# Delta-rule attention and two MLP stages on one core: output products held over the group boundary, untransposed triangles, a Newton square root and a block-wise first inversion

## The chip, the cores and the metric

The kernel runs on one core of one Trainium2 chip. TensorE (PE), VectorE (DVE), ScalarE (ACT), GpSimd (POOL) and the DMA queue of SyncE (SP) work side by side and wait for each other through semaphores. The metric is the device time of one execution in microseconds; of several runs the median is taken.

## The reference, cut to what matters

The inputs are q, k and v of 4 batches x 8 heads x 768 steps x 48 numbers, and a factor beta per step. The attention is a delta rule with a 48x48 state per head; its output goes through a gated MLP (384 to 1536 to 384, SiLU gate) and then a second MLP (384 to 2048 to 384, ELU):

```
k_n = k / (norm(k) + 1e-6)
for t in range(768):
    y[t]  = q[t] @ state
    state = state + beta[t] * outer(k_n[t], v[t] - k_n[t] @ state)
x   = y as [3072, 384]
x   = (silu(x @ w_gate) * (x @ w_val)) @ w_out
out = elu(x @ w_in) @ w_out2
```

## The kernel before, in words

**Groups.** The 3072 tokens are cut into 12 groups of 256: two batches x 128 steps, so 16 (batch, head) pairs `u` of 128 steps each. The 128 steps lie on the 128 partitions as four chunks `c` of 32. Inside a chunk the delta rule is solved at once: with A the strictly lower triangle of -beta k k^T, (I - A) is inverted for all 16 x 4 chunks, and only the states go from chunk to chunk.

**Attention of a group**, by function: `norm` (L162) squares k on POOL into `ain`, sums, and takes 1/(norm + 1e-6) with a Sqrt on ACT, a Newton-like correction and two reciprocals on DVE; `nkn` scales k by it. `trans` (L195) transposes q and k on PE, `kb` (POOL) scales k by -beta into `gr`, `gram` (L203) multiplies them and masks the result into `gr`. `inversion` (L219) transposes the triangles into `ain` in 32x32 blocks, eliminates row by row over 31 levels on DVE (L248 multiplies, L255 adds, a large level cut in two), transposes back into `ain` (`back`, L263), and copies the four chunks by ACT into `zt` (L270), where two 32x32 blocks stand on the diagonal of a 64x64 one. `xstep` (L276) multiplies by these inverses: 32 products of 64x64 with 96 columns. `gstep` (L286) makes the factors of the chunks in all four banks `at0` to `at3`, emptied by ACT (L298) and DVE (L299); `chain` carries the states, `yall` and `xtr` give the group's x in two parts `xh` and `xl`.

**First MLP of a group.** `gv1(g, f)` (L461) for the 12 slices f: 18 matmuls (L445) into one of the two banks `gv`, SiLU on ACT (L466), a multiply on DVE (L467) into `tb`, and a split into a high and a low part `hb` (ACT L345, DVE L348). `out1(g, f)` (L473) adds the slice to the one accumulator `acc` with 9 matmuls (L479); after slice 11 ACT empties `acc` (L486) into two `hb` buffers, from where DMAs write `x2d`.

**Order.** `moe1` (L611) writes the group's list: `out1` comes `LAG` = 2 slices after its `gv1`, and what is held at the end of a group is flushed there. `merge` (L590) mixes that list with the attention of the next group (and the inversion of the one after it), by the weights that stand with each step; what attention has goes over the first `ATT` = 0.85 of the list. The framework's planner then lays out each engine's queue, where a step that is ready in its model goes ahead of one that isn't; on the chip each engine works its queue in order. Group 0 has its attention, and the decoding of its weights (`decode`, integer and bit work on ACT, DVE and POOL), ahead of any MLP work. The second MLP (`h2`, `out2`) follows group 11; `t2` names the buffers in which its weights are decoded.

Of the kernel before, what the change touches and what calls it, by code (L numbers as in the profile page):

```python
# [11 lines left out]
I32 = mybir.dt.int32  # L12
# [9 lines left out]
def delta_moe_kernel(ctx: ExitStack, tc: tile.TileContext, q, k, v, beta,  # L22
# [9 lines left out]
    nc = tc.nc  # L32
# [28 lines left out]
    xl = {}  # L61
    NHB = 3
    NTB = 2

    ident = T("ident", [128, 128])
    strict = T("strict", [128, 32])
    zd = T("zd", [128, 2, 16])
    nbt = T("nbt", [128, NI, B * H])
# [10 lines left out]
    sm = [T(f"sm{n}", [128, 16]) for n in range(5)]  # L79
    neg1 = T("neg1", [128, 1])  # L80
# [24 lines left out]
    def emit_consts():  # L105
        make_identity(nc, ident)
        V.memset(neg1, -1.0)
        G.memset(strict, 1.0)
        for r in range(4):
            s = strict[32 * r:32 * r + 32, :]  # L110
            G.affine_select(out=s, in_=s, compare_op=ALU.is_ge, fill=0.0, base=-1,
                            pattern=[[1, 32]], channel_multiplier=-1)

        fl = sm[0][:, 0:1]
        V.tensor_reduce(out=fl, in_=ident.rearrange("p (r h m) -> p h r m", r=4, h=2)[:, 1],
                        op=ALU.add, axis=AX.XY)

        V.tensor_copy(zd[:, 1, :], fl.to_broadcast([128, 16]))
        V.tensor_scalar(out=zd[:, 0, :], in0=zd[:, 1, :], scalar1=-1.0, scalar2=1.0,
                        op0=ALU.mult, op1=ALU.add)  # L120

    def emit_zero():
        V.memset(kp[:, :, D:64], 0.0)
        V.memset(qp[:, :, D:64], 0.0)
        G.memset(zt, 0.0)
        G.memset(st[0:32], 0.0)
# [35 lines left out]
    def norm(g):  # L162
        i, b0 = ax_of(g)
        sq = ain[:, 0:768].rearrange("p (u d) -> p u d", d=D)
        ss, s, r, t, w = sm
# [15 lines left out]
    def nkn(g, a):  # L181
        u = slice(a * 8, a * 8 + 8)
        kk = kp[:, u, 0:D]
        V.tensor_tensor(out=kk, in0=kk, in1=sm[4][:, u].unsqueeze(2).to_broadcast([128, 8, D]),
                        op=ALU.mult)
        A.copy(out=R[:, u, 0:D], in_=kk)
# [31 lines left out]

    def inversion():  # L219
        lst = []  # L220
        an = ain.rearrange("p (l j) -> p l j", l=32)

        def start(n):
            def f():
# [3 lines left out]
                if n == 0:  # L228
                    z = buf['z'] = TT("z", [128, 32, 16])
                    G.memset(z, 0.0)  # L230
                    V.tensor_copy(win(z[:, 0:1, 0:1], [[16, 2], [33, 16]]), zd)
            return f
        lst += [start(n) for n in (3, 2, 1, 0)]

        def step(l):
            c0 = l // 2
# [19 lines left out]
            return [mul, add]  # L256
        for l in range(31, 0, -1):
            lst += step(l)

        def back():  # L260
            z = buf['z']
            t = ain[:, 0:512]
            V.transpose(out=t.rearrange("p (u i two) -> p i two u", u=16, two=2),  # L263
                        in_=z.rearrange("p a i -> p i a"))
        lst.append(back)

        def spread(r):
            def f():
                q0 = slice(32 * r, 32 * r + 32)
                A.copy(out=zt[q0, :, 32 * (r % 2):32 * (r % 2) + 32],  # L270
                       in_=ain[q0, 0:512].rearrange("p (u i) -> p u i", u=16))
            return f
        return lst + [spread(r) for r in range(4)]
# [280 lines left out]
    def attention(g, nx):  # L554
# [22 lines left out]
        if nx + 1 < NB:  # L577
            st1.append((0, lambda: load_q(nx + 1)))
        inv = inversion()
        inv = [(INV / len(inv), x) for x in inv]  # L580
# [30 lines left out]
    def moe1(g, before, after):  # L611
# [20 lines left out]
    POOL = 0  # L632
    CUT = 40
    LAG = 2
    LAG2 = 2
# [44 lines left out]
    def emit_all():  # L680
# [10 lines left out]
        for n in range(6, NW - 2):  # L691
            first.insert(1 + n - 6, (0, lambda n=n: load_w(n, src1(n))))
        inv = inversion()
        buf['dt'] = TT("dt", [128, 2, 2, DM], I32)
# [26 lines left out]
        late = []  # L721
        t2 = ("gr", "st", "zt", "dt")

# [64 lines left out]
```

## Time and profile before

| what | value |
|---|---|
| three runs | 1307.21, 1311.82 and 1316.99 us (median 1311.82) |
| profiled execution, first to last instruction (its span) | 1301.1 us |
| median less that span | 10.7 us |
| PE busy, PEld busy, DVE busy, ACT busy, POOL busy | 1162.0, 1078.5, 821.8, 608.6, 129.9 us |
| TensorE clock granted, mean | 0.949 |
| first MLP begins, group 11 ends, last instruction | 88.3, 880.9, 1301.1 us |

The profile gives no time of its own for the profiled execution beside its span, so the median stands in for it. The busy shares are averages over very different stages: 88 us of attention and decoding without MLP work, groups 0 to 11 up to 880.9 us, and the second MLP. They don't say which wait ends last in a stage; the rows below do.

### The profile page before, as it was taken

What the parts mean: (1) busy time and instruction counts of PE and PEld (TensorE: products, weight loads), DVE (VectorE), ACT (ScalarE), POOL (GpSimd) and SP (SyncE); (2) the same over time, 40 slices, a digit from 0 to 9 for tenths busy, and PEclk for the clock granted to TensorE, in tenths of its full rate; (3) what the DMA queues carried; (4) which work ended last, traced back from release to release, by engine and by line L of the source; (5) the groups of instructions that cost most, each with busy time, mean ns of one, the idle gap of its engine ahead of it and who ended that gap; (6) DMA issues with size and microseconds to landing.
All of it is one profiled execution on the core that took longest, in us unless ns stands there. A gap on an engine that the chain in (4) does not pass through costs nothing.

```text
span 1301.1 us, 31342 instructions
## 1 busy us (share of the span) xinstructions
PE 1162.0 (89%) x13086; PEld 1078.5 (83%) x13086; DVE 821.8 (63%) x2709; ACT 608.6 (47%) x1181; POOL 129.9 (10%) x106
## 2 busy tenths in 40 slices
PE   2473999898989898989898989989899999999998
PEld 1363889898888898989888989978689899899897
DVE  6799585848484858585848574467964545454443
ACT  7554534343425252535353524457754545454443
POOL 4353100000000000000000000031300000000000
PEclk9866798889999999999999999989999999999999
DMA  9530202020202020202020100373010101000000
GB/s 298 160 81 1 38 14 39 13 39 10 43 2 51 2 50 2 51 2 50 7 46 2 26 11 5 125 251 104 1 49 1 49 1 49 1 33 1 25 1 25
DMA packets 106815, 57.16 MB, mean 44 GB/s; under 512 B 76945, under 2 KB 101521, under 8 KB 106673
## 3 DMA queue, kind: packets, MB, share of 16 engines
q1 hardware_dynamic: 106672, 55.16, 16.7%
q8 instruction: 102, 1.67, 0.5%
q14 instruction: 41, 0.33, 0.1%
HBM read 45.71 MB, written 9.44 MB: 42 GB/s over the span
## 4 chain that ended last, share of the span: by engine, by line
PE 57%; DVE 34%; ACT 4%; issue 3%; DMA 1%; POOL 1%; SPq 0%; DVEq 0%; ACTq 0%; POOLq 0%
PE gv L445 14%; DVE z L255 7%; DVE ain L248 7%; PE acc L531 7%; PE at L531 7%; PE at L514 7%; PE gv L514 7%; PE acc L479 5%; PE at L294 4%; DVE w L404 2%; PE at L281 2%; DVE hb L348 2%; DVE tb L467 2%; DVE ain L227 2%; PE at L312 2%
## 5 line engine op out<-in xcount | busy, mean ns | idle before, releaser
L445 PE MATMUL gv<-xh,w 128*128 128x256 f32 x1728 | 295.9, 295 | 23.6 <-DVE tb L467 22.9
L445 PEld LDWEIGHTS gv<-xh,w 128*128 128x128 f32 x1728 | 248.9, 200 | 29.4 <-DVE tb L467 24.0
L479 PE MATMUL acc<-hb,w 128*128 128x256 f32 x1296 | 194.9, 298 | 37.6 <-ACT hb L345 34.7
L479 PEld LDWEIGHTS acc<-hb,w 128*128 128x128 f32 x1296 | 172.2, 199 | 45.5 <-ACT hb L345 36.7
L445 PE MATMUL gv<-xl,w 128*128 128x256 f32 x864 | 160.6, 295 | 1.5 <-DVE xl L348 1.5
L466 ACT ACTIVATE tb<-gv 128x256 f32<-128x256 f32 x144 | 54.9, 382 | 216.4 <-PE gv L445 216.0
L467 DVE TENSOR_TENSOR tb<-gv,tb 128x256 f32<-128x256 f32 x144 | 60.7, 422 | 127.6 <-ACT tb L466 126.7
L445 PEld LDWEIGHTS gv<-xl,w 128*128 128x128 f32 x864 | 131.7, 202 | 2.9 <-DVE xl L348 1.7
L345 ACT CAST hb<-tb 128x256 fp32r<-128x256 f32 x144 | 58.4, 406 | 146.8 <-DVE tb L467 146.2
L255 DVE TENSOR_TENSOR z<-z,ain 128x60 f32<-128x60 f32 (+32 forms) x696 | 122.5, 214 | 1.3
L248 DVE TENSOR_TENSOR ain<-z,ain 128x60 f32<-128x60 f32 (+32 forms) x696 | 122.3, 207 | 1.2
L348 DVE TENSOR_TENSOR hb<-tb,hb 128x256 fp32r<-128x256 f32 x144 | 76.7, 533 | 42.7 <-ACT hb L345 41.3
L521 DVE SCALAR_TENSOR_TENSOR hb<-at,hb 128x512 f32<-128x512 f32 x48 | 33.2, 691 | 84.5 <-ACT hb L520 84.5
L521 DVE SCALAR_TENSOR_TENSOR hb<-gv,hb 128x512 f32<-128x512 f32 x48 | 33.1, 690 | 80.2 <-ACT hb L520 72.5
L294 PE MATMUL at<-gr,R 32*96 32x80 f32 x1536 | 75.3, 276 | 8.7 <-DVE w L299 4.4
L294 PEld LDWEIGHTS at<-gr,R 32*96 32x96 f32 x1536 | 64.9, 179 | 19.0 <-DVE w L299 4.6
L520 ACT ACTIVATE hb<-hb,neg 128x512 f32<-128x512 f32 x96 | 69.4, 723 | 2.8
L518 ACT ACTIVATE hb<-at 128x512 f32<-128x512 f32 x48 | 28.6, 595 | 87.6 <-PE at L514 87.6
L518 ACT ACTIVATE hb<-gv 128x512 f32<-128x512 f32 x48 | 28.6, 596 | 85.3 <-PE gv L514 85.0
L281 PE MATMUL at<-R,zt 64*64 64x96 f32 x768 | 38.6, 254 | 27.5 <-ACT zt L270 27.4
L519 ACT ACTIVATE hb<-hb 128x512 f32<-128x512 f32 x96 | 60.6, 632 | 2.7
L281 PEld LDWEIGHTS at<-R,zt 64*64 64x64 f32 x768 | 35.8, 140 | 29.7 <-ACT zt L270 28.2
(174 smaller groups left out, 2154.6 us busy)
## 6 DMA issues: line engine op xcount, KB each, us to landing
w<-in_moe_w_out_dram SPq DMA_DIRECT2D x28, 384.0 KB, 6.6
w<-in_moe_w_in_dram SPq DMA_DIRECT2D x16, 384.0 KB, 5.6
kp<-in_k_dram SPq DMA_DIRECT2D x12, 384.0 KB, 5.4
qp<-in_q_dram SPq DMA_DIRECT2D x12, 384.0 KB, 4.3
w<-in_moe_w_gate_dram SPq DMA_DIRECT2D x12, 384.0 KB, 7.8
w<-in_moe_w_val_dram SPq DMA_DIRECT2D x12, 384.0 KB, 8.0
R<-in_v_dram SPq DMA_DIRECT2D x24, 192.0 KB, 2.6
x2d<-hb SPq DMA_DIRECT2D x12, 256.0 KB, 2.1
```

What stands on the lines that cost most here:

```text
L248: V.tensor_tensor(out=t, in0=z[:, l:l + 1, x:y].to_broadcast([128, l, y - x]), in1=an[:, l, 0:l].unsqueeze(2).to_broadcast([128, l, y - x] ...
L255: V.tensor_tensor(out=z[:, 0:l, x:y], in0=z[:, 0:l, x:y], in1=t, op=ALU.add)
L281: nc.tensor.matmul(p[r:r + 64, j], lhsT=zt[r:r + 64, 4 * n + j, :], rhs=R[r:r + 64, 4 * n + j, :], start=True, stop=True, skip_group_check ...
L294: nc.tensor.matmul(ps_[c][0:96, s * 80:s * 80 + 80], lhsT=R[t, u, :], rhs=gr[t, u, 0:80], start=True, stop=True, skip_group_check=True)
L348: (e2 or V).tensor_tensor(out=lo, in0=src, in1=hi.bitcast(F32), op=ALU.subtract)
L445: nc.tensor.matmul(dst, lhsT=wt[:, a_, kk * 128:(kk + 1) * 128], rhs=xx[:, kk, :], start=(n == 0), stop=(n == 3 * KD - 1))
L467: V.tensor_tensor(out=s, in0=p[:, TB:2 * TB], in1=s, op=ALU.mult)
L479: nc.tensor.matmul(o, lhsT=w[:, a_, d * 128:(d + 1) * 128], rhs=hh[:, b_, :], start=(f == 0 and n == 0 and d != 1), stop=(f == F1 - 1 and ...
L514: nc.tensor.matmul(p, lhsT=W[f][:, 0, a_, kk * 128:(kk + 1) * 128], rhs=x2[n][b_][:, kk, :], start=(m == 0), stop=(m == 3 * KD - 1))
L520: A.activation(out=r, in_=r, func=ACTF.Identity, bias=neg1, scale=1.0)
L521: V.scalar_tensor_tensor(out=r, in0=p, scalar=0.0, in1=r, op0=ALU.max, op1=ALU.add)
L531: nc.tensor.matmul(ob4[t], lhsT=hh[:, b_, t * 128:(t + 1) * 128], rhs=w[:, a_, :], start=(f == 0 and m == 0), stop=(f == F2 - 1 and m == 2))
```

## The change

1. **Held products.** `moe1` flushes what it holds only in the last group. So `out1(g, 10)` and `out1(g, 11)` now stand in group g + 1, behind its slices 0 and 1, and `acc` is emptied there. `NHB` is 4 in place of 3, for the slices that are live over the boundary.
2. **Inverted triangles where they stand.** `back` already leaves the inverses in `ain`, one 32x32 block for each of the 64 chunks; `zt` becomes a view of `ain`, the four copies (L270) and the clearing of the old `zt` go, and `xstep` makes 64 products of 32x32 in place of 32 of 64x64. `norm`, which writes `ain`, now has to wait for `xstep`.
3. **Newton square root.** The Sqrt on ACT goes; DVE starts from an integer guess and makes three Newton steps: 13 small DVE instructions in place of 6.
4. **Block-wise inversion in group 0.** There the two 16x16 halves of each triangle are inverted in the same 15 levels (30 instructions in all), and the part under them comes from two products on PE (`join1`, `join2`) with a DVE step between and an ACT copy behind.
5. **Smaller things.** `zd` is two columns in place of 32, `eye` holds four 32x32 identities, and the decode buffers `t2` are three in place of four.

```diff
-    NHB = 3
+    NHB = 4
...
-    zt = T("zt", [128, 16, 64])
+    zt = ain[:, 0:512].rearrange("p (u j) -> p u j", u=16)
...
     def norm(g):
...
-        A.activation(out=s, in_=ss, func=ACTF.Sqrt)
-
-        V.tensor_scalar(out=r, in0=s, scalar1=1e-18, scalar2=None, op0=ALU.max)
-        V.reciprocal(out=r, in_=r)
-        V.tensor_tensor(out=t, in0=ss, in1=r, op=ALU.mult)
-        V.tensor_tensor(out=t, in0=t, in1=s, op=ALU.add)
-        V.tensor_scalar(out=t, in0=t, scalar1=-0.5, scalar2=-1e-6, op0=ALU.mult, op1=ALU.add)
-        V.reciprocal(out=w, in_=t)
+        V.tensor_scalar(out=s.bitcast(I32), in0=ss.bitcast(I32), scalar1=-0.5,
+                        scalar2=float(0x5f3759df), op0=ALU.mult, op1=ALU.add)
+        for _ in range(3):
+            V.scalar_tensor_tensor(out=r, in0=s, scalar=-0.5, in1=ss, op0=ALU.mult, op1=ALU.mult)
+            V.tensor_tensor(out=r, in0=r, in1=s, op=ALU.mult)
+            V.scalar_tensor_tensor(out=s, in0=r, scalar=1.5, in1=s, op0=ALU.add, op1=ALU.mult)
+        V.tensor_tensor(out=r, in0=ss, in1=s, op=ALU.mult)
+        V.tensor_scalar(out=r, in0=r, scalar1=-1.0, scalar2=-1e-6, op0=ALU.mult, op1=ALU.add)
+        V.reciprocal(out=s, in_=r)
...
+        def halves(l):
+            c0 = l // 2
+            n = 8 - c0
+            t = win(ain[:, 512:513], [[8, 2], [32, l], [1, n]])
+
+            def mul():
+                z = buf['z']
+                V.tensor_tensor(out=t, in0=win(z[:, l:l + 1, c0:c0 + 1], [[264, 2], [0, l], [1, n]]),
+                                in1=win(ain[:, 32 * l:32 * l + 1], [[528, 2], [1, l], [0, n]]),
+                                op=ALU.mult)
+
+            def add():
+                z = win(buf['z'][:, 0:1, c0:c0 + 1], [[264, 2], [16, l], [1, n]])
+                V.tensor_tensor(out=z, in0=z, in1=t, op=ALU.add)
+            return [mul, add]
+        for l in range(15 if blocked else 31, 0, -1):
+            lst += (halves if blocked else whole)(l)
 
         def back():
...
+            if blocked:
+                V.transpose(out=d1t, in_=d1)
+
+        def join1():
+            p = buf['jp'] = nxt(atb, "at").rearrange("p (u j) -> p u j", u=16)
+            for u in range(16):
+                for c in range(C):
+                    r = 32 * c
+                    nc.tensor.matmul(p[r:r + 32, u],
+                                     lhsT=gr[r:r + 16, u, 80:112],
+                                     rhs=d1t[r:r + 16, u], start=True, stop=True,
+                                     skip_group_check=True)
+            v = buf['v'] = TT("z", [128, 16, 32])
+            V.scalar_tensor_tensor(out=v, in0=p, scalar=low[:, 0:1],
+                                   in1=eye.unsqueeze(1).to_broadcast([128, 16, 32]),
+                                   op0=ALU.mult, op1=ALU.add)
+
+        def join2():
+            p = nxt(atb, "at").rearrange("p (u j) -> p u j", u=16)
+            for u in range(16):
+                for c in range(C):
+                    t = slice(32 * c, 32 * c + 32)
+                    nc.tensor.matmul(p[t, u], lhsT=buf['v'][t, u], rhs=d1[t, u], start=True,
+                                     stop=True, skip_group_check=True)
+            A.copy(out=zt, in_=p)
+        return lst + ([back, join1, join2] if blocked else [back])
...
     def xstep():
         for n in range(4):
             p = nxt(atb, "at")[:, 0:384].rearrange("p (n w) -> p n w", n=4)
             for j in range(4):
-                for r in (0, 64):
-                    nc.tensor.matmul(p[r:r + 64, j], lhsT=zt[r:r + 64, 4 * n + j, :],
-                                     rhs=R[r:r + 64, 4 * n + j, :], start=True, stop=True,
+                for c in range(C):
+                    t = slice(32 * c, 32 * c + 32)
+                    nc.tensor.matmul(p[t, j], lhsT=zt[t, 4 * n + j, :],
+                                     rhs=R[t, 4 * n + j, :], start=True, stop=True,
                                      skip_group_check=True)
             A.copy(out=R[:, 4 * n:4 * n + 4, :], in_=p)
...
-        while held:
+        while held and g == NB - 1:
             put(1, held.pop(0), 1.0, out1)
...
-        t2 = ("gr", "st", "zt", "dt")
+        t2 = ("gr", "st", "dt")
```

## Rows read from the trace of the kernel before

**Rows 1.** Page, part 1: busy time of each engine, its share, instructions.
```profile
PE 1162.0 (89%) x13086; PEld 1078.5 (83%) x13086; DVE 821.8 (63%) x2709; ACT 608.6 (47%) x1181; POOL 129.9 (10%) x106
```
**Rows 2.** Stretches, groups 6, 10, 11: width; PE, PEld, DVE, ACT, POOL busy; clock; DMA.
```profile
516.90:581.50 64.60, 60.03 (x922) 56.96 (x922) 43.97 (x193) 26.63 (x63) 4.62 (x6) 0.97 0.15 27
...
776.20:829.00 52.80, 52.71 (x760) 50.44 (x761) 20.36 (x57) 18.04 (x48) 0.00 (x0) 0.97 0.03 9
829.00:880.90 51.90, 46.04 (x357) 45.06 (x356) 31.56 (x41) 26.62 (x49) 11.14 (x6) 0.93 0.76 253
```
**Rows 3.** PE in order of time, group 6 and its end: start, us, count, [idle].
```profile
523.94 2.86 PE L281 MATMUL at<-R,zt 64*64 64x96 f32 x64
...
574.65 2.67 PE L479 MATMUL acc<-hb,w 128*128 128x256 f32 x18
...
581.53 2.41 PE L479 MATMUL acc<-hb,w 128*128 128x256 f32 x9 [4.09 <-ACT hb L345]
...
588.68 2.86 PE L281 MATMUL at<-R,zt 64*64 64x96 f32 x64
```
**Rows 4.** Chain of waits at that end: start, us, what.
```profile
576.98 1.08 DVE ain L263
...
578.77 0.63 ACT zt L270
579.41 0.38 ACT tb L466
```
**Rows 5.** PE's waits, 186 to 780 us: for whom, total, times, longest.
```profile
PE acc L479 <- ACT hb L345: 33.5, 9, 4.1
```
**Rows 6.** Chain of waits: gv products behind the first and last end; undisturbed ones.
```profile
255.54 5.13 PE gv L445 x35
...
778.34 7.04 PE gv L445 x53
...
865.77 2.16 PE gv L445 x18
```
**Rows 7.** PE in order of time, group 6: factors, transposes, triangles.
```profile
529.06 0.92 PE L294 MATMUL at<-gr,R 32*96 32x80 f32 x32
...
543.04 1.03 PE L200 MATMUL at<-ident,qp 128*128 128x128 f32 x8
543.91 1.04 PE L200 MATMUL at<-ident,kp 128*128 128x128 f32 x8
...
549.15 1.73 PE L210 MATMUL at<-kq 48*32 48x64 f32 x128
```
**Rows 8.** Groups of instructions: busy, mean ns | idle before, releaser.
```profile
L201 ACT COPY kq<-at 128x512 f32<-128x512 f32 x48 | 25.7, 588 | 0.7 <-DVE tb L467 0.5 <-PE at L200 0.3
...
L166 POOL TENSOR_TENSOR ain<-kp 128x768 f32<-128x768 f32 x11 | 16.1, 1465 | 18.8 <-ACT zt L270 18.8
...
L168 ACT ACT_TABLE_LOAD x11 | 14.1, 1283 | 0.2
...
L248 DVE TENSOR_TENSOR ain<-z,ain 128x60 f32<-128x60 f32 (+32 forms) x696 | 122.3, 207 | 1.2
...
L521 DVE SCALAR_TENSOR_TENSOR hb<-at,hb 128x512 f32<-128x512 f32 x48 | 33.2, 691 | 84.5 <-ACT hb L520 84.5
```
**Rows 9.** DVE in order of time in group 0's attention.
```profile
12.83 0.18 DVE L170 TENSOR_SCALAR sm<-sm 128x16 f32<-128x16 f32 x1 [4.91 <-ACT sm L168]
...
14.25 1.03 DVE L184 TENSOR_TENSOR kp<-kp,sm 128x384 f32<-128x384 f32 x2
...
28.13 0.19 DVE L248 TENSOR_TENSOR ain<-z,ain 128x31 f32<-128x31 f32 x1
...
43.68 1.06 DVE L263 STREAM_TRANSPOSE ain<-z 128x512 f32<-128x512 f32 x1
```
**Rows 10.** PE in order of time in group 0's attention.
```profile
17.18 2.73 PE L210 MATMUL at<-kq 48*32 48x64 f32 x128 [0.34 <-ACT kq L201]
46.87 6.34 PE L281 MATMUL at<-R,zt 64*64 64x96 f32 x64 [26.95 <-ACT zt L270]
```

More of the change, by code (lines that the diff above doesn't have):

```diff
@@ L66, in delta_moe_kernel @@
     strict = T("strict", [128, 32])
-    zd = T("zd", [128, 2, 16])
+    zd = T("zd", [128, 2])
     nbt = T("nbt", [128, NI, B * H])
@@ L75, in delta_moe_kernel @@
     ain = T("ain", [128, 1024])
-    zt = T("zt", [128, 16, 64])
+    zt = ain[:, 0:512].rearrange("p (u j) -> p u j", u=16)
+    eye = T("eye", [128, 32])
+    low = zd[:, 1:2]
     st = T("st", [128, B, DM])
     sv = T("sv", [128, 2, C - 1, DM])
-    sm = [T(f"sm{n}", [128, 16]) for n in range(5)]
+    sm = [T(f"sm{n}", [128, 16]) for n in range(3)]
     neg1 = T("neg1", [128, 1])
@@ L112, in emit_consts @@
                             pattern=[[1, 32]], channel_multiplier=-1)
-        fl = sm[0][:, 0:1]
-        V.tensor_reduce(out=fl, in_=ident.rearrange("p (r h m) -> p h r m", r=4, h=2)[:, 1],
+        for r in range(4):
+            q0 = slice(32 * r, 32 * r + 32)
+            V.tensor_copy(eye[q0], ident[q0, q0])
+        V.tensor_reduce(out=low, in_=ident.rearrange("p (r h m) -> p h r m", r=4, h=2)[:, 1],
                         op=ALU.add, axis=AX.XY)
-        V.tensor_copy(zd[:, 1, :], fl.to_broadcast([128, 16]))
-        V.tensor_scalar(out=zd[:, 0, :], in0=zd[:, 1, :], scalar1=-1.0, scalar2=1.0,
+        V.tensor_scalar(out=zd[:, 0:1], in0=low, scalar1=-1.0, scalar2=1.0,
                         op0=ALU.mult, op1=ALU.add)
@@ L124, in emit_zero @@
         V.memset(qp[:, :, D:64], 0.0)
-        G.memset(zt, 0.0)
         G.memset(st[0:32], 0.0)
@@ L183, in nkn @@
         kk = kp[:, u, 0:D]
-        V.tensor_tensor(out=kk, in0=kk, in1=sm[4][:, u].unsqueeze(2).to_broadcast([128, 8, D]),
+        V.tensor_tensor(out=kk, in0=kk, in1=sm[1][:, u].unsqueeze(2).to_broadcast([128, 8, D]),
                         op=ALU.mult)
@@ L216, in gram, with inversion @@
                         op=ALU.mult)
-    def inversion():
+    def inversion(blocked):
         lst = []
         an = ain.rearrange("p (l j) -> p l j", l=32)
+        d1 = ain[:, 0:512].rearrange("p (u j) -> p u j", u=16)
+        d1t = ain[:, 512:1024].rearrange("p (u j) -> p u j", u=16)
         def start(n):
@@ L230, in f, with whole @@
                     G.memset(z, 0.0)
-                    V.tensor_copy(win(z[:, 0:1, 0:1], [[16, 2], [33, 16]]), zd)
+                    V.tensor_copy(win(z[:, 0:1, 0:1], [[16, 2], [33, 16]]),
+                                  zd.unsqueeze(2).to_broadcast([128, 2, 16]))
             return f
         lst += [start(n) for n in (3, 2, 1, 0)]
-        def step(l):
+        def whole(l):
             c0 = l // 2
@@ L256, in step @@
             return [mul, add]
-        for l in range(31, 0, -1):
-            lst += step(l)
-        def back():
[L261 to L272, printed above, removed]
@@ L273, in inversion @@
-        return lst + [spread(r) for r in range(4)]
+        def halves(l):
[11 more added lines that the diff above has]
+            return [mul, add]
@@ new lines, in inversion @@
+        for l in range(15 if blocked else 31, 0, -1):
+            lst += (halves if blocked else whole)(l)
+        def back():
+            V.transpose(out=ain[:, 0:512].rearrange("p (u i two) -> p i two u", u=16, two=2),
+                        in_=buf['z'].rearrange("p a i -> p i a"))
+            if blocked:
[13 more added lines that the diff above has]
+                                   op0=ALU.mult, op1=ALU.add)
@@ L578, in attention @@
             st1.append((0, lambda: load_q(nx + 1)))
-        inv = inversion()
+        inv = inversion(False)
         inv = [(INV / len(inv), x) for x in inv]
@@ L632, in delta_moe_kernel @@
     POOL = 0
+    LAG = 2
     CUT = 40
-    LAG = 2
     LAG2 = 2
@@ L692, in emit_all @@
             first.insert(1 + n - 6, (0, lambda n=n: load_w(n, src1(n))))
-        inv = inversion()
+        inv = inversion(True)
         buf['dt'] = TT("dt", [128, 2, 2, DM], I32)
```

2 lines of the change are left out of this document (1 added, 1 removed).

## The prediction

> **What bounds the kernel now.** I read the page's first part, then a table of stretches, then PE's own order of time around the end of a group, then the chain of waits there. PE is busy for 89% of the span [rows 1], an average over unlike stages. By stretch [rows 2], group 6 takes 64.6 us with 60.0 of PE, while group 10, which has an attention but no inversion beside it, is 52.7 busy of 52.8. So PE can be filled, and something keeps it from that in the other groups. PE's order shows what [rows 3]: behind slice 11's gv product it does the output products of slices 9 and 10, up to 577 us, and then stands still for 4.09 us, until slice 11's high part is there (ACT, L345). What follows is slow: nine output products in 2.41 us, about what 18 took just before, because TensorE has dropped to the lower of its two clock levels behind the gap (group 6 has a mean of 0.97 [rows 2]).
>
> The chain of waits tells why slice 11 is late [rows 4]. DVE finishes the inversion for the next group (L263, to 578.06), ACT copies its chunks into `zt` (L270, 0.63 us each), and the SiLU of slice 11 (L466, 579.41) stands between these copies in ACT's queue, its cast behind them. The last slice waits for an inversion that it has nothing to do with, and PE waits for the slice because the flush leaves it nothing else. The same wait comes at nine ends (groups 1 to 9): 33.5 us in all [rows 5].
>
> **Held products.** They remove no work. They put two gv products (18 in 2.16 us, 0.12 each [rows 6]) and older output products between slice 11's gv product and its output product. From 574.65 us PE now goes through out1 of slice 9 (9 x 0.12 = 1.08), gv of the next group's slice 0 (2.16) and out1 of slice 10 (1.08), to 579.0, and then has `xstep` or slice 1's gv. Slice 10 was ready before 577, since PE did its product then; the inversion is done at 578.06; slice 11's `tb` needs one SiLU and one multiply behind that. Nothing that PE comes to should still be missing, though by little. In a steady period the margin is wider: from one `xstep` to the next are 588.68 - 523.94 = 64.7 us [rows 3]; less 4.09 idle, less 1.33 (2.41 - 1.08) and 0.6 (the gv products behind: 4.81 for 35 that take 4.20) this is 58.7 us of PE, while from `xstep` to the end of the next inversion are 578.06 - 523.94 = 54.1. PE stays the bound with some 4.5 us to spare.
>
> What is given back is 33.5 us of idle time and the lower clock behind it: 2.41 against 1.08 at seven ends and 2.15 at an eighth, 10.4 us; and the gv products behind (nine pieces from 5.13 to 7.04, the last with 53 products, against 0.12 each [rows 6]), 5.4 us. Sum **49.3 us**.
>
> What the hold adds: (a) ACT now empties `acc` (two copies, 512 and 256 columns, some 0.9 us by [rows 8]) between out1 of slice 11 and, one gv product of 2.16 us later, the new group's first output product. It costs nothing if ACT takes it at once; behind two or three copies for `gstep` in ACT's queue it would cost PE about 1 us. (b) The x2d writes move on SP past the next k load, whose buffer is long free: 0. (c) In group 11 two more output products stand between the first weight loads, and group 10 loses them: 0, as group 11 idles 5.9 us anyway [rows 2]; the third part of its decode buffers that is left out falls under the same idle time, 0, with those 5.9 us again as the bound if it doesn't.
>
> **Untransposed triangles.** Four ACT copies a group go, 2.5 us, and a hop. Beside the hold they are worth nothing more on the path, as PE reaches `xstep` after the inversion's end. `xstep` becomes 128 records (each fp32 product is two) of 32x32 in place of 64 of 64x64. The 64 take 2.86 us [rows 3], some 43.6 ns each without the last one's tail. From below: four 32-column tiles ran 128 records of 64 columns in 1.73 us [rows 7], so 2.6 for 96. From above: four row tiles of 32 ran 32 records of 80 columns in 0.92 us [rows 7], so 4.4 for 128 of 96. I take no change, since the row nearest to it is `xstep` itself, whose two diagonal tiles already overlap: 43.6 ns a record, where a full-width fp32 record of 128 columns takes 109 (eight from 543.04 to 543.91 [rows 7]) and 96 columns would take 82. Bounds: -0.2 and +1.6 a group, -2 and +19 over twelve.
>
> A rule of the Trainium skill speaks against this edit: TensorEngine Tiling (Array Packing), section Gotcha 1: PSUM Pressure, says that different row tiles cannot access the same PSUM bank at one time. By it `xstep` would go as in rival 3; the 43.6 ns of this trace, two row tiles into one bank, don't agree with it.
>
> `norm` has a new wait. Its squares (POOL, 1.47 us [rows 8]) go into `ain`, where `zt` now lies, so they wait for `xstep`; behind them in POOL's queue stand the mask that `gram` needs and `kb`. With `xstep` at T: squares from T + 2.9, sum to about T + 5.3, root to T + 8, scaled k by T + 9.3. The transposes of k stand on PE 20 us behind `xstep` (543.91 against 523.94 [rows 3, 7]), so 10 us of other PE work cover it. But these 4.8 us of DVE now fall among the `gstep`s (from T + 5), whose banks DVE helps to empty, and PE could wait up to all of it. I take 0.5 us a group together with (a), 5.5 in eleven groups; bounds 0 and 3 a group.
>
> **Newton root.** ACT loses the root and two table loads (1.28 us each [rows 8]). DVE gains seven instructions of about 0.22 us (six took 14.25 - 12.83 = 1.42 [rows 9]), 1.5 us a group. In the MLP groups both lie off the path. In group 0 DVE stood still for 4.91 us before 12.83 [rows 9]; 13 Newton instructions from 7.9 end at 10.8 in place of 14.25: 3.5 us gained.
>
> **Block-wise inversion, group 0.** The levels took 43.68 - 28.13 = 15.5 us [rows 9]. Now 30 instructions at 0.21 us [rows 8] and 0.03 between: 7.2 us, 8.3 saved. Added behind: a second transpose (1.06 [rows 9]), two sets of 128 records (1.4 to 2.7 us each, by 2.73 at the low clock [rows 10] with half the columns; 2.0), a combine (0.69) and a copy (0.59) [rows 8], and four hops of some 0.1: 6.8 us. Removed: 2.1 us from the transpose's end (44.74) to `xstep` (46.87 [rows 10]). Net 8.3 - 6.8 + 2.1 = 3.6, with the root 7 us at `xstep`. After it DVE still decodes weights up to the first MLP slice, which isn't shortened; of the 7 I take 5 as arriving there, bounds 0 and 8.
>
> **Sum.** Against the execution's span: 1301.1 - 49.3 - 5 + 5.5 + 0 = 1252.3 us. The median lies 10.7 above the span, so **1263 us**, 3.7% faster.
>
> **The rivals.**
>
> 1. *New waits eat half.* `gstep` with DVE's norm steps among them and the late emptying of `acc` cost 3 us a group in place of 0.5: 11 x 2.5 = 27 more, 1290 us. For it: `gstep` takes all four banks, and PE has no second set. Against: gv products stand among them, and norm has 10 us of slack.
> 2. *The stall moves to `xstep`.* The planner lays out slice 11's multiply behind the inversion, and `xstep` or slice 1's gv ahead of work that is ready; PE still waits some 2 us at each end and the clock still drops. Then only the 2.5 us of ACT copies come off at nine ends, 22 us, with 5 from group 0: 1285 us.
> 3. *Slower: row tiles in turn.* If the four row tiles of `xstep` can't write one bank together, 128 records of 82 ns take 10.5 us in place of 2.8, 92 us in twelve groups: 1355 us. From 54 ns a record on it takes all that the rest gives (49 us over 1536 records). For it speaks no row; against it the 43.6 ns.
> 4. *The hold does nothing*, because the inversion, not the flush, sets the period. Against: 54.1 us against 58.7. It would leave group 0's 5 us: 1307.
>
> **How the numbers follow.** Forecast 0.70, rival 1 0.13, rival 2 0.08, rival 3 0.04, rival 4 0.05. Low end: group 0 gives 8, `xstep` -2, no new waits, 1252, and 5 for the scatter of the runs: 1247. High end: rivals 1 and 2, with 2 of scatter: 1292. About 1% (13 us; the three runs lie 10 apart) is what a measurement here can tell from no change. Faster by that: forecast and rivals 1 and 2, 0.90 of their 0.91, since rival 1 ends near the bound; within it, rival 4, 0.05; slower, rival 3 and the like, 0.05.
>
> **What would show it.** Right: no 4 us gap on PE at the ends, periods of 59 us from `xstep` to `xstep`, the clock at its upper level through the ends, `xstep` records at about 22 ns, no table load before norm, group 0's `xstep` near 40 us. Wrong: PE waiting at L479 for L486, at L294 for L299, or `xstep` of 4 us and more.

## The result, and the profile after

The changed kernel takes **1262.08 us** (median of four runs, 1261.85 to 1264.82) beside 1309.51 us for the kernel before in the same comparison (four runs, 1300.85 to 1316.99): a ratio of 0.9653, 95% interval 0.9595 to 0.971. The forecast was 1263 us.

The agreement is luck for a good part. The profiled execution after has a span of 1263.1 us and a time of 1264.82 us, so only 1.7 us lie outside a span, not the 10.7 us that the prediction added. Those were the scatter of the kernel before: in a later comparison its runs went from 1301.26 us (clock 0.953) to 1311.02 us (clock 0.940), each 1.7 to 1.8 us above its own span, so that by the same offset the profiled execution of 1301.1 us would have taken some 1302.8 us, less than any of the three runs of the median. Span against span, 1252.3 us were forecast and 1263.1 measured: 38.0 us gained, not 48.8. A trace shows one execution of several, which by its own time can lie off the median: 2.7 us above it in the kernel after, 6.4 us above it in `e8`, 3.2 us below it in `e6`.

The page of the kernel after, part 1, answers to [rows 1]. PE is busy for 92% of a shorter span:

```profile
PE 1156.2 (92%) x14110; PEld 1075.0 (85%) x14110; DVE 808.1 (64%) x2712; ACT 551.9 (44%) x1101; POOL 129.6 (10%) x105
```

Line numbers have moved: `gv1` is L484 (before L445), `out1` L518 (L479), its SiLU and multiply L505 and L506 (L466, L467), the casts and splits L384 and L387 (L345, L348), `xstep` L320 (L281), its copies L323 (L284), `gstep` L333 (L294), its evacuation L337 on ACT and L338 on DVE (L298, L299), the squares, the sum and the root L169, L170 and L171 to L179, the scaling L188 (L184), the emptying of `acc` L525 (L486). In `e4`, `e5` and `e8` all lines behind the root stand two lower.

From the first gv product to the end the kernel takes 32.5 us less (1212.8 us from 88.3 us before, 1180.2 us from 82.86 us after). Nearly all the change lies between the triangle steps of groups 1 and 11, ten periods. View of stretches (width; busy time of PE, PEld, DVE, ACT and POOL with their instructions; granted clock; share and rate of DMA), before:

```profile
133.70:785.30 651.60, 605.40 (x9153) 574.18 (x9153) 436.54 (x1925) 266.44 (x627) 46.21 (x49) 0.95 0.14 25
```

After, and then from the last triangle step to the end:

```profile
127.90:741.60 613.70, 592.18 (x9786) 563.90 (x9786) 433.97 (x1995) 213.64 (x553) 47.08 (x50) 0.96 0.12 26
741.60:1263.10 521.50, 501.30 (x3147) 454.61 (x3146) 267.83 (x429) 266.05 (x442) 31.49 (x16) 0.99 0.14 45
```

PE's idle time there (width less busy) falls from 46.2 to 21.5 us, its busy time by 13.2 us at a higher clock. Without the 33.5 us of [rows 5], 12.7 us of idle time would have been left. PE's waits after, from 186 to 780 us, answer to [rows 5]:

```profile
PE at L333 <- DVE lc L338: 14.2, 9, 1.6
```

The wait for the last slice is gone, and a new one has come in nine groups: `gstep` waits for DVE. It is one of the signs of being wrong that the prediction named (L294 for L299, by the old lines). PE in order of time around one `xstep` (start, us, count, idle time), against [rows 3]:

```profile
489.20 1.24 PE L518 MATMUL acc<-hb,w 128*128 128x256 f32 x9
...
492.57 1.24 PE L518 MATMUL acc<-hb,w 128*128 128x256 f32 x9
493.74 2.84 PE L320 MATMUL at<-R,ain 32*32 32x96 f32 x128
...
498.86 0.92 PE L333 MATMUL at<-gr,R 32*96 32x80 f32 x32
499.71 1.33 PE L518 MATMUL acc<-hb,w 128*128 128x256 f32 x9
502.62 2.40 PE L333 MATMUL at<-gr,R 32*96 32x80 f32 x32 [1.58 <-DVE lc L338]
504.95 1.01 PE L484 MATMUL gv<-xh,w 128*128 128x256 f32 x3
```

Output products and gv products now alternate up to `xstep` without a gap. Then the second `gstep` waits 1.58 us and takes 2.40 us, and the three gv products behind it take 1.01 us. In group 6 of the kernel before, the same two pieces stand without a wait and are shorter:

```profile
531.17 1.83 PE L294 MATMUL at<-gr,R 32*96 32x80 f32 x32
532.94 0.62 PE L445 MATMUL gv<-xh,w 128*128 128x256 f32 x3
```

The granted clock was 1.00 from 498.8 to 502.6 us and 0.77 from 502.5 to 510 us. The chain of waits there says what DVE was at (start, us, what):

```profile
493.81 2.82 PE at L320 x128
...
496.69 1.48 POOL ain L169
...
498.20 0.97 DVE sm L170
...
500.20 0.33 DVE tb L506
...
502.17 0.04 DVE sm L179
...
502.34 0.61 DVE lc L338 x3
502.95 0.46 DVE kp L188
503.42 0.21 DVE lc L338
```

The squares go into `ain`, where `zt` lies, so they start when `xstep` ends. The sum and thirteen root operations follow. In DVE's queue they stand ahead of the `lc` additions that give `gstep` its banks back, and around slice work (`tb`, L506): ACT's cast of that slice waits for it, and ACT's own copies for `gstep` (L337) are queued behind the cast. From `xstep`'s end to the first addition are 5.7 us.

### The profile page after: what moved, and what is told of

It is laid out like the page before. It is cut to its first block, busy times and chain, and to the rows that moved or that the text cites. A ratio compares the mean times of both kernels' runs of the same rounds, so it can differ in the third digit from the quotient of the medians.

```text
span 1263.1 us, 33318 instructions
## 1 busy us (share of the span) xinstructions
PE 1156.2 (92%) x14110; PEld 1075.0 (85%) x14110; DVE 808.1 (64%) x2712; ACT 551.9 (44%) x1101; POOL 129.6 (10%) x105
## 4 chain that ended last, share of the span: by engine, by line
PE 76%; DVE 13%; DMA 3%; issue 3%; ACT 2%; SPq 1%; POOL 1%; DVEq 0%; ACTq 0%
PE gv L484 22%; PE acc L518 11%; PE acc L570 7%; PE at L570 7%; PE gv L553 7%; PE at L553 7%; PE at L333 4%; PE at L351 3%; PE at L320 3%; DVE w L443 2%; PE at L204 1%; PE at L364 1%; PE at L214 1%; POOL ain L169 1%; DVE z L262 1%
## 5 line engine op out<-in xcount | busy, mean ns | idle before, releaser
L484 PE MATMUL gv<-xh,w 128*128 128x256 f32 x1728 | 299.3, 298 | 22.5 <-DVE tb L506 21.9
L484 PEld LDWEIGHTS gv<-xh,w 128*128 128x128 f32 x1728 | 250.4, 202 | 29.3 <-DVE tb L506 22.9
L518 PE MATMUL acc<-hb,w 128*128 128x256 f32 x1296 | 187.2, 289 | 4.1 <-DVE hb L387 2.5
L518 PEld LDWEIGHTS acc<-hb,w 128*128 128x128 f32 x1296 | 166.6, 193 | 8.2 <-DVE hb L387 3.0
L484 PE MATMUL gv<-xl,w 128*128 128x256 f32 x864 | 158.1, 293 | 2.6 <-DVE xl L387 2.5
L505 ACT ACTIVATE tb<-gv 128x256 f32<-128x256 f32 x144 | 55.0, 383 | 211.3 <-PE gv L484 211.0
L384 ACT CAST hb<-tb 128x256 fp32r<-128x256 f32 x144 | 58.4, 406 | 185.8 <-DVE tb L506 185.6
L484 PEld LDWEIGHTS gv<-xl,w 128*128 128x128 f32 x864 | 131.2, 202 | 3.2 <-DVE xl L387 2.7
L506 DVE TENSOR_TENSOR tb<-gv,tb 128x256 f32<-128x256 f32 x144 | 60.4, 420 | 112.2 <-ACT tb L505 111.4
L262 DVE TENSOR_TENSOR z<-z,ain 128x60 f32<-128x60 f32 (+22 forms) x638 | 112.9, 214 | 1.1
L255 DVE TENSOR_TENSOR ain<-z,ain 128x60 f32<-128x60 f32 (+22 forms) x638 | 112.7, 207 | 1.4
L333 PE MATMUL at<-gr,R 32*96 32x80 f32 x1536 | 75.4, 277 | 22.9 <-DVE lc L338 19.0
L333 PEld LDWEIGHTS at<-gr,R 32*96 32x96 f32 x1536 | 63.7, 177 | 34.4 <-DVE lc L338 20.6
L387 DVE TENSOR_TENSOR hb<-tb,hb 128x256 fp32r<-128x256 f32 x144 | 68.9, 479 | 28.0 <-ACT hb L384 27.9
L553 PE MATMUL gv<-lc,w 128*128 128x512 f32 x144 | 41.8, 400 | 3.6 <-DVE hb L560 3.6
L443 DVE TENSOR_SCALAR w<-w 128x768 uint8<-128x768 uint8 x34 | 41.5, 1240 | 1.1 <-ACT w L428 1.1
```

The source lines that it names most:

```text
L255: V.tensor_tensor(out=t, in0=z[:, l:l + 1, x:y].to_broadcast([128, l, y - x]), in1=an[:, l, 0:l].unsqueeze(2).to_broadcast([128, l, y - x] ...
L262: V.tensor_tensor(out=z[:, 0:l, x:y], in0=z[:, 0:l, x:y], in1=t, op=ALU.add)
L333: nc.tensor.matmul(ps_[c][0:96, s * 80:s * 80 + 80], lhsT=R[t, u, :], rhs=gr[t, u, 0:80], start=True, stop=True, skip_group_check=True)
L387: (e2 or V).tensor_tensor(out=lo, in0=src, in1=hi.bitcast(F32), op=ALU.subtract)
L443: V.tensor_scalar(out=by[:, :, :, 3], in0=by[:, :, :, 7], scalar1=128, scalar2=None, op0=ALU.bitwise_and)
L484: nc.tensor.matmul(dst, lhsT=wt[:, a_, kk * 128:(kk + 1) * 128], rhs=xx[:, kk, :], start=(n == 0), stop=(n == 3 * KD - 1))
```

## The experiments

All were run beside the kernel before (medians 1302.45 to 1304.37 us). "After" in a diff is the changed kernel; `e2` and `e7` start from the kernel before.

**e1_flush: the hold undone.**
```diff
-        while held and g == NB - 1:
+        while held:
```


> The kernel after with one edit undone: each group again flushes its last two output products at its own end. Theory (the held products are the gain): at each of the nine group ends TensorE waits about 4 us for the last split of the slice again, and runs its next matmuls at the low clock behind it; the time goes up by the term that the trace of before gives for this, about 40 to 49 us, to 1302 to 1311 us, and the rows of the second output product show some 30 us of idle time again. Rival (the gain came from the triangles, the root and the freed copies, and the hold only moves a wait): 1262 to 1275 us, and the idle time in front of the output products comes back while some other wait of the same size goes.

1291.2 us, ratio 0.9895 (0.9865 to 0.9926): the hold is worth 29 us here, less than the theory's 40 to 49, more than the rival's 13. The wait at the ends came back short. PE's waits from 186 to 780 us:

```profile
PE at L333 <- DVE lc L338: 14.2, 9, 1.6
PE acc L518 <- ACT hb L384: 11.4, 9, 1.5
```

11.4 us over nine ends, not the 33.5 us of [rows 5]: with no `zt` copies ahead of the SiLU and the cast on ACT [rows 4], PE stands still for 1.3 us at an end in place of 3.7, and at the end that the chain of waits was read for, the slice waits for DVE's last transpose alone (its multiply, L506, follows the transpose at 505.09 us). The untransposed triangles and the hold mend the same gap, the first by two thirds, the second wholly.

**e2_hold_alone: the kernel before with the hold, three slice buffers.**
```diff
-        while held:
+        while held and g == NB - 1:
```


> The kernel before with the hold alone: the last two output products go into the next group; old triangles, old square root, whole inversion, three decode buffers, and only three buffers for the split slices instead of four, as the old triangles' buffer stays and the fourth has no room. Theory (the hold is the gain by itself): the 4 us gaps go, 1265 to 1280 us, of which up to 10 us lies in the third buffer's double use at the ends (ScalarE's copy of the second half of the sums waits for the DMA of the first). Rival (the stall moves to the triangle step when the slices run on, as the four copies of the triangles and the table loads of the root stand late on ScalarE): TensorE waits 2 to 3 us for the triangle copies in each of ten groups, 1285 to 1300 us.

1260.38 us, 0.9659 (0.9629 to 0.969): **44.0 us from the hold by itself**, as much as the whole change gives (ratio 0.9653), and quicker than the theory's 1265. The rival's wait at `xstep` doesn't come. The third buffer's double use shows in the chain of waits:

```profile
323.17 0.61 ACT hb L486
...
323.80 3.79 DMA x2d<-hb
...
327.67 0.38 ACT hb L486
...
328.07 1.70 DMA x2d<-hb
...
329.85 0.41 ACT hb L345
```

ACT's second copy out of `acc` waits for the first one's DMA, the next slice's cast for the second's, and `gstep`'s copies stand behind them on ACT; PE waits 1.5 us at a `gstep` in this group, and 7.0 us at nine `gstep`s in all (L294 for L299). The other three parts with the fourth buffer therefore bring nothing together (1260.4 against 1262.1 us). So the next question is which of them loses.

**e3_own_squares: the squares in the scratch tile.**
```diff
-        sq = ain[:, 0:768].rearrange("p (u d) -> p u d", d=D)
+        sq = TT("z", [128, 16, D])
```


> The kernel after with the squares of the norm written into the scratch tile of the inverse (1 KB wider) rather than into the tile that now also holds the triangles, so that they need not wait for the triangle step. Theory (the time over the sum of the prediction is the norm's chain behind the triangle step): the 12 waits of the gstep matmuls for VectorE's lc, 19.0 us in all in the kernel after, fall below 5 us and the low clock behind them goes too, 1235 to 1250 us. Rival (the gstep would wait anyway for its four banks and the evacuation, whatever the norm does): within 4 us of 1262 us.

1243.08 us, 0.9526 (0.9496 to 0.9556), as the theory had it: `gstep`'s waits for `lc` leave the list of the largest from 186 us on.

**e4_sqrt: the old root.** `norm` has `A.activation(..., func=ACTF.Sqrt)` and the six VectorE operations again.

> The kernel after with the old square root: one Sqrt on ScalarE, with its table loads, and the six small VectorE operations instead of the twelve. Theory of the prediction (the root is off the path in the groups with MLP work, 3.5 us on it in group 0): 1263 to 1268 us. Rival (as the squares now wait for the triangle step, the root would stand on ScalarE between the triangle's and the gstep's evacuations, with two table loads of 1.28 us each and the wait for the squares): TensorE waits 2 to 4 us more in each of ten groups at the gstep, 1282 to 1300 us, and the Newton root is then what makes the shared tile cheap.

1237.35 us, 0.9493 (0.9449 to 0.9536): neither. The old root is **24.7 us better**. DVE in order of time behind one `xstep` of `e4`:

```profile
482.90 0.95 DVE L170 TENSOR_REDUCE sm<-ain 128x16 f32<-128x768 f32 x1 [3.63 <-POOL ain L169]
484.14 0.17 DVE L172 TENSOR_SCALAR sm<-sm 128x16 f32<-128x16 f32 x1 [0.28 <-ACT sm L171]
...
485.55 0.56 DVE L186 TENSOR_TENSOR kp<-kp,sm 128x384 f32<-128x384 f32 x1
486.03 0.42 DVE L504 TENSOR_TENSOR tb<-gv,tb 128x256 f32<-128x256 f32 x1
486.36 0.47 DVE L336 TENSOR_TENSOR lc<-at,kq 48x128 f32<-48x128 f32 x2
```

From the sum's start to the first `lc` addition are 3.46 us, where the kernel after has 4.14 (498.20 to 502.34). PE waits 0.58 us here in place of 1.58, and what follows runs at the upper clock. The ten periods of `e4`, with PE idle for 10.9 us in place of 21.5, and the wait:

```profile
128.10:718.70 590.60, 579.74 (x9787) 551.50 (x9786) 424.91 (x1925) 240.28 (x583) 47.06 (x50) 0.99 0.12 27
...
486.69 1.10 PE L331 MATMUL at<-gr,R 32*96 32x80 f32 x16 [0.58 <-DVE lc L336]
```

The periods give 23.1 us; another 4.8 us of this trace's gain lie in the last stretch (see below). ACT takes the table loads at 481.85 and 484.12 us, the first of them while it would wait for the squares anyway.

**e5_sqrt_own_squares: both edits.**

> The kernel after with both edits that helped alone: the old square root on ScalarE and the squares in the scratch tile. Theory (each edit shortens the same chain of squares, sum, root and lc behind the triangle step, which is worth 1.6 us of TensorE's idle time and the low clock behind it in each group): once the chain is off the path a second shortening brings nothing, 1232 to 1243 us. Rival (the two are separate gains of 25 and 19 us): 1215 to 1225 us.

1231.1 us, 0.944 (0.94 to 0.9481): 0.9 us under the theory's range and far from the rival's; 44 us of separate gains come to 31. The `gstep`s' waits for `lc` from 130 to 720 us are down to 1.2 us, and the periods in the middle are 57.9 us. PE itself is the bound: it is idle for 6.1 us of the ten periods.

**e6_one_iteration: a shorter Newton chain.**
```diff
-        for _ in range(3):
+        for _ in range(1):
```


> The kernel after with one Newton iteration in place of three, so the norm is computed less exactly; six VectorE operations of about 0.21 us are left out of each group's chain. Theory (the three iterations cost as VectorE's operations in line between the sum of squares and the gstep's lc): 1235 to 1245 us, as with the old square root, or below it, and the waits of the gstep for lc fall from 19.0 us to under 9. Rival (the old square root gained by the other order into which the planner then lays the queues, not by the length of the chain): 1256 to 1264 us.

1256.37 us, 0.9635 (0.9589 to 0.9681): the rival's range. My theory of the length fell: six operations less on DVE (1.3 us a group) gave 5.7 us and left the waits, 13.5 us at nine `gstep`s from 186 to 680 us. DVE's order shows why:

```profile
494.75 0.25 DVE L179 RECIPROCAL sm<-sm 128x16 f32<-128x16 f32 x1
495.03 0.56 DVE L188 TENSOR_TENSOR kp<-kp,sm 128x384 f32<-128x384 f32 x1
495.51 0.42 DVE L387 TENSOR_TENSOR hb<-tb,hb 128x256 fp32r<-128x256 f32 x1
495.84 0.55 DVE L188 TENSOR_TENSOR kp<-kp,sm 128x384 f32<-128x384 f32 x1
496.31 0.87 DVE L338 TENSOR_TENSOR lc<-at,kq 48x128 f32<-48x128 f32 x4
```

Both scalings of k (0.55 us each) now stand ahead of the `lc` additions; in the kernel after both stood behind the first three of them. What was saved in the root went into work queued ahead. That makes the order the suspect, and `e9` and `e12` test it. The 5.7 us are not the whole story of the periods: by the trace, group 0's triangle step comes 4.2 us later (48.74 us), and the ten periods take 599.1 us for 613.7, with PE idle for 19.4 us (21.5 after) but busy for 579.7 (592.2). So PE worked faster behind gaps of nearly the same length; why the clock fell less often there is not shown.

**e7_hold_newton: the hold and Newton on the kernel before**, where `ain` is free before `xstep`.

> The kernel before with the hold and the Newton root, old triangles, whole inversion, three buffers: the squares do not wait for the triangle step here. It stands against 1260 us of the hold alone. Theory (Newton costs only because the squares wait for the triangle step in the shared tile): 1254 to 1262 us, 3.5 us of gain in group 0 included. Rival (the longer serial chain on VectorE costs about 2 us a group wherever it stands): 1272 to 1286 us.

1258.72 us, 0.9651 (0.9611 to 0.969): as the theory. Newton costs nothing (1.7 us less than `e2`) where the squares needn't wait for `xstep`.

**e8_sqrt_whole: hold, triangles and fourth buffer.** `e4` with `inversion(False)` in group 0.

> The kernel after with the old square root and with group 0's triangles inverted whole as before, so that the hold, the triangles and the fourth buffer are left of the change. It stands against 1237 us with the block-wise inversion and against 1260 us of the hold alone. Theory (the block-wise inversion is worth its 2.4 us at the triangle step of group 0 and no more): 1238 to 1242 us, and the triangles with the freed copies are worth some 20 us over the hold alone. Rival (group 0's first slices wait for decoded weights, so an earlier triangle step arrives nowhere): 1235 to 1238 us. A second rival (the 23 us between the two kernels lie in the block-wise inversion): about 1260 us.

1236.27 us, 0.9488 (0.9443 to 0.9532): the first rival's time, but not for its reason. The block-wise inversion brings nothing beside the old root (1237.35 with it), because group 0's triangle step isn't earlier by it: 46.74 us in `e4`, 45.68 us here. The triangles with the fourth buffer are worth **24.1 us over the hold alone**.

**e9_norm_behind: Newton kept, the order changed.** The norm's DVE work is queued behind the additions of the first two `gstep`s.
```diff
-        return [(0.4, lambda: (load_v(g, 0), load_v(g, 1), norm(g), nkn(g, 0), nkn(g, 1))),
+        def sums():
+            load_v(g, 0), load_v(g, 1)
+            with ExitStack() as es:
+                if g > 0:
+                    es.enter_context(tc.issue_after(behind[0]))
+                norm(g), nkn(g, 0), nkn(g, 1)
+        return [(0.4, sums),
```
Here `behind[0]` is the last VectorE instruction that the second `gstep` traced.

> The kernel after, Newton's root and the shared tile kept, with one more rule for the order of VectorE's queue: the norm's sum, root and scaling are queued behind the eight lc additions of the first two gsteps. Theory (what costs is that the norm's chain stands in VectorE's queue, waiting for the squares, ahead of the product of the slice and of the lc additions; its length alone is little): the gstep's waits for lc fall from 19.0 us to under 7 us, 1233 to 1244 us, with all three iterations. Rival (the chain has to be done somewhere in the group, so a later chain makes the inversion and the next triangle step late): TensorE waits at the triangle step for VectorE's last transpose, 1 to 3 us in each of ten groups, 1250 to 1270 us.

1248.26 us, 0.9573 (0.9533 to 0.9614): 13.8 us gained, short of the theory's range. The rival's wait at `xstep` doesn't come; the wait moved to the fourth `gstep`, 8.6 us at nine of them (L333 for L338, 0.96 us each), as the chain now stands ahead of the third one's additions.

**e10_whole: group 0 inverted whole.**
```diff
-        inv = inversion(True)
+        inv = inversion(False)
```


> The kernel after with group 0's triangles inverted whole, as before. It tells what the block-wise inversion brings in the kernel as it was changed. Theory of the prediction (5 us earlier at the first MLP slice by root and inversion, of which the inversion is 2 to 3.6 us): 1264 to 1266 us. Rival (the first slices wait for decoded weights and the gain is lost there): 1259 to 1263 us.

1258.92 us, 0.9667 (0.9617 to 0.9717): just under the rival's range and 3.2 us better than the change by medians. These come from two comparisons, and by ratio (0.9667 for 0.9653) it isn't better, so the times alone don't settle it; the theory's gain of 2 us or more is not there. The traces say more: the triangle step of group 0 stands at 42.88 us here and at 42.84 us in `e11`, and at 44.25 to 44.99 us in the five runs with the block-wise inversion and three Newton steps (`after`, `e1`, `e3`, `e9`, `e12`). At the first gv product little is left of that: 80.39 and 80.89 us, against 80.78 to 82.86 us. PE in order of time in group 0, `e10` (the second row is the triangle step, L320):

```profile
16.07 2.73 PE L214 MATMUL at<-kq 48*32 48x64 f32 x128 [3.16 <-ACT kq L205]
42.88 4.29 PE L320 MATMUL at<-R,ain 32*32 32x96 f32 x128 [24.08 <-DVE ain L284]
```

and the kernel after:

```profile
35.36 1.93 PE L294 MATMUL at<-ain,gr 16*32 16x32 f32 x128 [16.56 <-DVE ain L287]
38.16 1.18 PE L308 MATMUL at<-ain,z 32*32 32x32 f32 x71 [0.87 <-DVE z L299]
42.82 0.97 PE L308 MATMUL at<-ain,z 32*32 32x32 f32 x57 [3.48 <-issue]
44.50 3.09 PE L320 MATMUL at<-R,ain 32*32 32x96 f32 x71 [0.70 <-ACT ain L310]
47.79 2.39 PE L320 MATMUL at<-R,ain 32*32 32x96 f32 x56 [0.20 <-issue]
```

The block-wise levels end early, but the two joins take 9.1 us to `xstep`, with 3.48 us of it in the middle of `join2` in which PE waits for no other engine. All eight runs with the joins have this hole, always behind the 71st of the 128 records of `join2`, 2.66 to 3.48 us long. The DMA view of the hole (39.3 to 42.9 us, kernel after) shows a transfer that isn't the kernel's data, one of instructions:

```profile
q8 instruction: 1, 0.02, 1.8%
```

In all eight runs a 16 KB transfer of this queue ends within the hole (at 41.25 us here), and PE goes on 1.2 to 1.6 us behind its end. That PE waits there for its own instructions fits these rows; no run tests it.

**e11_best: what helped, together.** Hold, triangles, four buffers, own squares, Newton in group 0 alone, whole inversion.
```diff
+        if g == 0:
...
+        else:
+            A.activation(out=s, in_=ss, func=ACTF.Sqrt)
```


> The parts that helped, together: hold, triangles as inverted, four buffers, the squares in the scratch tile, the Newton root in group 0 alone and the old root on ScalarE in the eleven groups with MLP work, group 0's triangles inverted whole. Theory: 1231 us of the two edits together, less about 2 us each for Newton and for the whole inversion at the first MLP work (the triangle step of group 1 came 2.1 and 2.2 us earlier by them): 1226 to 1230 us. Rival (the first MLP slices wait for decoded weights, and what group 0 gains is lost there): 1230 to 1235 us.

**1227.79 us** (five runs, 1224.48 to 1229.8), 0.9408 (0.9362 to 0.9453): as the theory, and 34.3 us faster than the change. The periods in the middle are 57.9 us, as in `e5`.

**e12_norm_last: as e9, behind all four `gstep`s.**

> The kernel after with Newton's root and the shared tile, and the norm's operations on VectorE queued behind the lc additions of all four gsteps, not of two. Behind two the wait moved to the fourth gstep (0.96 us, ten times). Theory (the norm's chain costs only where it stands ahead of lc additions): no gstep waits over 0.6 us, 1235 to 1242 us, about the time with the old root. Rival (Newton's chain costs the same wherever it is put, as VectorE then has it ahead of the state additions or of the inversion): 1246 to 1256 us, with waits of the state products or of the triangle step in place of the gstep's.

1234.72 us, 0.9476 (0.9428 to 0.9523): 0.3 us under the theory's range, and with its waits. With all three iterations and the shared tile the order alone gives **27.4 us**. DVE in order of time behind one `xstep`, from the last `lc` additions on:

```profile
488.39 1.26 DVE L338 TENSOR_TENSOR l<-at,kq 48x128 f32<-48x128 f32 x4 [1.29 <-ACT l L337]
489.69 0.95 DVE L170 TENSOR_REDUCE sm<-ain 128x16 f32<-128x768 f32 x1
...
494.52 0.25 DVE L179 RECIPROCAL sm<-sm 128x16 f32<-128x16 f32 x1
```

PE's waits from 186 to 780 us, the largest first:

```profile
PE at L204 <- DVE kp L188: 4.3, 9, 0.5
...
PE at L333 <- DVE dt L338: 0.3, 1, 0.3
```

The same chain, 5.1 us long here with other work within it, now holds up only the transposes of k, by 0.5 us a group. In the 20 us around the triangle steps (2 us before their start to 18 us behind it) of groups 2 to 11 the granted clock is 1.00.

## Why the prediction was right, and where it was not

The time was right; the sum behind it was not. Two terms were wrong by over 20 us each, in opposite directions: the triangles were put at nothing and gave 24.1 us, and the norm with its new wait was put at 2 us and cost 22.6. That they cancel is luck, and so is that the 6.5 us by which the sum was still too hopeful were covered by the offset of 10.7 us, 9 too large. By medians of the experiments, each part on top of those above it:

| part | forecast, us | measured, us | from |
|---|---|---|---|
| hold | -49.3 | -44.0 | e2 against before |
| triangles, fourth buffer, old root | 0 | -24.1 | e8 against e2 |
| Newton | norm +5.5, group 0 -3.5 | +22.6 | e10 against e8 |
| block-wise inversion | the rest of group 0's -5 | +3.2 | after against e10 |
| sum | -48.8 | -42.3 | 1304.4 to 1262.1 |

The rows follow the experiments, so norm's new wait stands with Newton, though with the old root it was there too (in `e8` it is part of -24.1). Another order of the parts gives other numbers: on top of all the rest the hold is worth 29.1 us (`e1`). And the medians come from several comparisons, in which the kernel before took 1302.45 to 1304.37 us, and 1309.51 us beside the kernel after; the 3.2 us of the block-wise inversion lie within that scatter.

**The hold** was read rightly from [rows 3 to 6]: PE stood still for the last slice because the flush left it nothing else to do. Alone it gives 44.0 of 49.3 us, although having only three buffers brings waits of its own (7.0 us at `gstep`). The forecast's (a), ACT emptying `acc` late, is small: 1.6 us at four output products in `e2` (L479 for L486), 1.5 us once in the kernel after, in group 11. Rivals 2 and 4 fell: from group 2 on PE doesn't wait at `xstep`, and the hold does something.

**The triangles** were valued at nothing beside the hold, and that step failed. With the fourth buffer they give 24.1 us. Between `e2` and `e8` the first triangle step with MLP work comes 6.1 us earlier (133.9 and 127.8 us), and the ten periods shrink from 609.4 to 596.1 us: the idle time from 15.7 to 10.8, the busy time from 593.7 to 585.3 at a clock of 0.98 for 0.97. These traces show 18.3 us of the 24.1, as the one of `e8` is of a longer execution. The wait for the third buffer's DMA in `e2` is one part of this; how much belongs to the ACT copies that went was not separated, since the fourth buffer has no room beside the old `zt`.

**`xstep`** was rightly taken as unchanged: 128 records in 2.84 us, 22 ns each, where the 64 took 2.86. Rival 3 fell by the row. The Trainium skill's rule in TensorEngine Tiling (Array Packing), section Gotcha 1: PSUM Pressure, which stood behind it, doesn't hold for this pattern: four row tiles, each with its own column tile, write one bank together.

**Norm's new wait** was seen and named, down to the 4.8 us of DVE among the `gstep`s, and then priced at 0.5 us a group where 27.4 / 11 = 2.5 us was right (`e12`): rival 1 in its place and nearly in its size. The price was set by the cover of 10 us up to the transposes of k. It should have been set by the queue: DVE's rows stand in the order of its queue, and behind the waiting sum stood the `lc` additions for which PE waits. The wait itself is 1.58 us; the rest goes with the clock. In the same 20 us around the triangle steps of groups 2 to 10, in each of which PE has this gap, the granted clock of the kernel after is 0.80 to 1.00, in seven of the nine 0.91 or less; in group 11, without the gap, it is 1.00.

**Newton** was called off the path in the groups with MLP work. It is on it, because the change itself had put the squares behind `xstep`: without that (`e7`) it costs nothing, and queued last (`e12`) nothing either. Group 0's term was right: between `e8` and `e10` `xstep` comes 2.8 us earlier with it (45.68 and 42.88 us) and the first gv product 3.4 us (83.79 and 80.39 us), 3.5 forecast.

**The block-wise inversion** saved on DVE what was forecast: the last transpose's start falls from 41.70 us (`e10`) to 33.47. What is added behind it was mis-sized: 6.8 us forecast, 9.9 us measured from the first transpose's end to `xstep` (34.56 to 44.50; 46.87 in [rows 10]). Less the hole of 3.48 us in `join2` these would be 6.4, near the forecast, so it is the hole that the sum lacked. In this execution the order of ACT's queue alone would have brought the same delay: the decoding ahead of the copy behind `join2` ends at 43.87 us, and the copy follows at once. Of the 8.2 us saved nothing is left, and 1.6 us are lost at `xstep`. The 5.4 us by which group 0 came earlier (88.31 to 82.86) agree with the 5 forecast only as a sum of other parts: 4.7 us came with the triangles and the smaller edits (88.45 in `e2`, 83.79 in `e8`), where the sum had only the copies' 2.1, 3.4 with Newton, and 2.5 were lost again.

**The last stretch**, from the triangle step of group 11 on, takes 5.7 us more than before (515.8 to 521.5). Of the 82 more of PE's records in it, 64 are the step's own and 18 are one more slice of gv products, 2.2 us: the step stands one slice earlier in the list. The other 3.5 us were not forecast, as (c) was put at nothing, and their cause is open. The stretch takes 519.8 to 521.5 us in the six runs with the hold, four buffers and Newton in every group (`after`, `e3`, `e6`, `e9`, `e10`, `e12`), and 515.9 to 516.9 us in the four with the old root in the groups with MLP work (`e4`, `e5`, `e8`, `e11`), though most of it is the second MLP, which has no norm. So some 3 us of Newton's 22.6 stand there (519.8 in `e10`, 516.9 in `e8`) and are not the wait at `gstep`.

## What to carry to other kernels

When a new buffer reuse makes an operation wait, list what is queued behind that operation on its engine and who waits for that; the slack of the operation's own result prices only a part of it. Two edits that mend one stall aren't additive, and an edit that costs nothing in one kernel can cost 23 us beside another edit that moved its start. Before an expensive chain is rewritten, try queuing it later: here the order of one queue was worth as much as going back to the old root (27.4 and 24.7 us).

## What the runs showed of the hardware

What the lower clock costs behind a gap can be more than the gap. In the ten periods the kernel after and `e4` do the same work with nearly the same records (9786 and 9787): the idle time differs by 10.7 us, and PE's busy time by another 12.4 us, with a granted clock of 0.96 and 0.99. Behind gaps of 1.58 us (kernel after) the clock stood at its lower level for a while in seven of nine groups, behind gaps of 1.50 us (`e6`) in four of nine, behind gaps of 0.58 us (`e4`) in three of nine. So the gap's length alone doesn't tell whether it falls.

Four row tiles of 32 in one PSUM bank ran at 22 ns a record of 96 columns, half of the 43.6 ns of two row tiles of 64: the time of the whole step didn't change with the tiles' size (2.84 and 2.86 us).

The two joins, 256 small matmul records in close order, had a hole of 2.66 to 3.48 us in all eight runs that contain them, and each hole held the end of a 16 KB instruction transfer.

The kernel before took 1298.39 to 1317.94 us over all comparisons, with each run's time some 1.7 us above its own span: a span can't be subtracted from a median of other runs.
